# Unread products of the identity in TensorE's pauses of the first two blocks

## The chip, the cores and the metric

The kernel runs on one core of a Trainium2 chip. The metric is the time of one execution on the device in microseconds, median of three runs; lower is better. Besides, one execution was recorded by the hardware profiler, and all times of single instructions come from that one.

## What is computed

The reference has two halves. The first is attention within chunks of 64 positions; the second is a gated feed-forward layer on all 4608 rows.

```python
scores = q_c @ k_c.T / sqrt(64)              # per batch, head and chunk of 64
attn = softmax(scores)                        # exp, row sum + 1e-9, divide
x = (attn @ v_c)                              # laid out as 4608 rows of 512
g = x @ w_gate                                # 512 -> 1536
y = (g * sigmoid(g) * (x @ w_val)) @ w_out    # 1536 -> 512
```

There are 8 batches, 8 heads, 576 positions and a head dimension of 64.

## The kernel before, in words

The 4608 rows are worked in nine blocks of 512 (`NB`, `N`). For each block the kernel makes the attention output x, transposed, as four tiles of 128x512 (one for each pair of heads), and then for each of twelve slices f of 128 of the 1536 hidden columns a gate product, a value product and a projection back. To keep the accuracy of f32 at a better rate, each factor is split into a high and a low part in the type fp32r, and each product is made of three (`three`, lines 271 to 275: high times low, low times high, high times high). A gate or value product of one slice is thus twelve products of 128x128 by 128x512, recorded under lines 273, 274 and 275; a projection is twelve more under lines 318 to 320.

The weights come in as pairs of words and are first brought into f32 by a handful of steps on ScalarE and VectorE (`scale`, `sign`, `shift`, `below`, `power`, `weigh`, `join`, lines 74 to 97), then split by `upper` (line 124, ScalarE) and `lower` (line 129, VectorE).

The attention of the first two blocks, a0 and a1, is what matters here:

- `scores` (line 180) makes 64x64 products in plain f32 on quarters of the array (line 192) into two PSUM tiles; VectorE takes the row maximum (line 197) and subtracts it (line 198).
- `exponents` (line 201) is one ScalarE instruction for two pairs of heads; `normalize` (line 206) is four VectorE instructions, lines 208 to 211.
- `turn_by_pe` (line 213) turns a pair's probabilities by four 128x128 transposes with the identity (line 216) into a tile of ps_a, and ScalarE copies it out (line 217).
- `columns` (line 219) multiplies with v in 64x64 products (line 226) into a tile `px`.
- `split` (line 54) makes high (line 56, ScalarE) and low (line 57, VectorE) of px: these are the tiles xh and xl, which the gate's products read.

`by_pe` (line 395) does `turn_by_pe` and `columns` for two pairs. The identity `ident` (line 51) is filled by GpSimd at the start.

The order of the instructions on TensorE, ScalarE, VectorE and on the load queue is the order of the program text: lines 361 and 377 switch the planner off. So TensorE goes through lines 402 to 463 as they stand: scores of a0 in two halves, transposes and columns of a0 in two halves, first half of the scores of a1, the gate product of a0, second half of the scores of a1, the value product of a0, transposes and columns of a1 in two halves, gate and value products of a1, the first projection. An engine starts an instruction when the one ahead of it in its queue has started and its own data is there.

PSUM is divided by lines 46 to 48: `ps_gv` with two banks for gate and value, `ps_o` with four for the projection's sums (also lent to the scores' second half and to px in the first two blocks), `ps_a` with two for the attention.

Of the kernel before, what the change touches and what calls it, by code (L numbers as in the profile page):

```python
# [8 lines left out]
F32 = mybir.dt.float32  # L9
# [10 lines left out]
P = 128  # L20
# [15 lines left out]
def attn_then_gated_ffn(ctx: ExitStack, tc: tile.TileContext, qk, v, wgv, wo, out):  # L36
    nc = tc.nc
# [8 lines left out]
    ps_gv = ctx.enter_context(tc.tile_pool(name="ps_gv", bufs=2, space=bass.MemoryType.PSUM))  # L46
    ps_o = ctx.enter_context(tc.tile_pool(name="ps_o", bufs=T, space=bass.MemoryType.PSUM))
# [2 lines left out]
    const.tile([P, 96], F32, name="pad")  # L50
    ident = const.tile([P, P], F32, name="ident")
    make_identity(nc, ident)

    def split(src, hi, lo, engine=None):

        nc.scalar.copy(out=hi, in_=src)  # L56
        (engine or nc.vector).tensor_tensor(out=lo, in0=src, in1=hi.bitcast(F32), op=ALU.subtract)  # L57
# [225 lines left out]
    def product(a, f, g):  # L283
        ps = ps_gv.tile([P, N], F32, name="ps_gv")
        for kk in range(NK):
            three(ps, (w_hi[f][:, g, kk], w_lo[f][:, g, kk]), a.x[kk], kk, NK)
        return ps

    def gate(a, f):
        pg = product(a, f, 0)  # L290
        h = hp.tile([P, N], F32, name="h")
        nc.scalar.activation(h, pg, AF.Silu, scale=2.0 ** -8)  # L292
        return h

    def value(a, f):
        return product(a, f, 1)
# [102 lines left out]


    w, o = up[0], down[0]
    a0.scores(q0[0], 0)
    a0.scores(q0[1], 2, pool=ps_o, tag="ps_o")
    e = [a0.exponents(p, 2) for p in (0, 2)]
    w.scale()
    a0.normalize(e[0])
# [15 lines left out]


    a1.scores(q1[0], 0)
    h0 = gate(a0, 0)
    a1.scores(q1[1], 2, pool=ps_o, tag="ps_o")
    pv0 = value(a0, 0)
    w = up[1]
    w.scale()
    e = [a1.exponents(p, 2) for p in (0, 2)]  # L430
# [187 lines left out]
```

## Time and profile before

| what | before |
|---|---|
| median of 3 runs | 989.31 us (988.85 to 989.68) |
| profiled execution | 988.99 us |
| its span, first to last instruction | 987.1 us |
| mean granted clock of TensorE | 0.991 |
| TensorE busy, products | 952.7 us (97%), 6232 records |
| TensorE busy, weight loads | 782.2 us, 6232 records |
| VectorE busy | 513.5 us (52%) |
| ScalarE busy | 337.7 us (34%) |

In rows of the profile PE stands for TensorE's products, PEld for its weight loads, DVE for VectorE, ACT for ScalarE, POOL for GpSimd. A row of the timeline has start, length in us, engine, line, operation, output<-inputs and count; in brackets stands how long the engine had been idle and what released it. A row of a group has the total busy time and the mean of one in ns. A row of a stretch has its length, then the busy time (and count) of PE, PEld, DVE, ACT and POOL, the granted clock of TensorE (1.00 is full), the DMA share and GB/s. Ends of products are modelled, so lengths of single products overlap; what counts is the distance between starts.

### The profile page before, as it was taken

The numbers are of one execution on the slowest core, as the hardware profiler recorded it, in microseconds if no ns is written. First come the engines' busy times: TensorE is split into PE (matmuls) and PEld (weight loads), VectorE is DVE, ScalarE is ACT, GpSimd is POOL, SyncE is SP. The second block draws the span as 40 slices with busy tenths as digits, with TensorE's granted clock in tenths as the row PEclk, the third lists the DMA queues.
The fourth block names the chain that finished last, engine by engine and source line by source line (L and its number), as shares of the span: only waits on it lengthen the run. The fifth ranks groups of instructions, "written<-read, shape, count | busy, mean of one in ns | idle before, by whom it ended". The sixth has DMA issues, their size and how long they took to land.

```text
span 987.1 us, 14517 instructions
## 1 busy us (share of the span) xinstructions
PE 952.7 (97%) x6232; PEld 782.2 (79%) x6232; DVE 513.5 (52%) x816; ACT 337.7 (34%) x523; POOL 0.7 (0%) x6
## 2 busy tenths in 40 slices
PE   4689999999999999999999999999999999999998
PEld 4577888876888888888888888888888888888886
DVE  6777777758447524662356345633564347522221
ACT  3455444434532223222332323233322332223222
POOL 0000000000000000000000000000000000000000
PEclk9799999999999999999999999999999999999999
DMA  9061333235240005010401030002100120001001
GB/s 362 14 234 38 134 147 141 92 112 160 80 136 1 22 1 150 1 23 1 150 0 23 1 112 39 22 1 92 58 20 4 29 79 1 22 1 43 0 1 43
DMA packets 45600, 63.85 MB, mean 65 GB/s; under 512 B 29664, under 2 KB 29664, under 8 KB 44000
## 3 DMA queue, kind: packets, MB, share of 16 engines
q1 hardware_dynamic: 38624, 50.34, 15.8%
q10 hardware_dynamic: 6912, 12.59, 3.4%
q8 instruction: 49, 0.80, 0.3%
q14 instruction: 15, 0.12, 0.0%
HBM read 50.33 MB, written 12.58 MB: 64 GB/s over the span
## 4 chain that ended last, share of the span: by engine, by line
PE 91%; DVE 4%; DMA 2%; ACT 2%; issue 1%; ACTq 0%; SPq 0%; DVEq 0%
PE ps_gv L273 20%; PE ps_gv L274 19%; PE ps_gv L275 19%; PE ps_o L318 9%; PE ps_o L319 9%; PE ps_o L320 9%; DMA qk_t<-in_qk 2%; PE ps_a L192 2%; PE ps_a L251 1%; PE px L226 1%; DVE z L208 1%; DMA out<-o_sb 0%; DVE s_sb L211 0%; DVE t L81 0%; DVE t L97 0%
## 5 line engine op out<-in xcount | busy, mean ns | idle before, releaser
L273 PE MATMUL ps_gv<-xl,w 128*128 128x512 f32 x864 | 341.1, 395 | 3.4 <-ACT h L292 2.1
L274 PE MATMUL ps_gv<-xh,w 128*128 128x512 f32 x864 | 338.1, 391 | 3.2 <-DVE w L129 3.2
L275 PE MATMUL ps_gv<-xh,w 128*128 128x512 f32 x864 | 337.9, 391 | 0.0
L299 DVE SCALAR_TENSOR_TENSOR h<-ps_gv,h 128x512 f32<-128x512 f32 x108 | 74.6, 690 | 359.3 <-PE ps_gv L275 359.3
L273 PEld LDWEIGHTS ps_gv<-xl,w 128*128 128x128 f32 x864 | 163.0, 189 | 39.3 <-ACT h L292 2.5
L274 PEld LDWEIGHTS ps_gv<-xh,w 128*128 128x128 f32 x864 | 163.1, 189 | 36.9 <-DVE w L129 3.8
L275 PEld LDWEIGHTS ps_gv<-xh,w 128*128 128x128 f32 x864 | 163.0, 189 | 34.2
L292 ACT ACTIVATE h<-ps_gv 128x512 f32<-128x512 f32 x108 | 64.5, 597 | 315.0 <-PE ps_gv L275 314.9
L318 PE MATMUL ps_o<-woh,hl 128*128 128x512 f32 x432 | 169.9, 393 | 2.2 <-DVE hl L57 2.1
L319 PE MATMUL ps_o<-wol,hh 128*128 128x512 f32 x432 | 169.0, 391 | 0.0
L320 PE MATMUL ps_o<-woh,hh 128*128 128x512 f32 x432 | 168.9, 391 | 0.0
L56 ACT CAST hh<-h 128x512 fp32r<-128x512 f32 x96 | 59.6, 621 | 183.4 <-DVE h L299 183.4
L318 PEld LDWEIGHTS ps_o<-woh,hl 128*128 128x128 f32 x432 | 81.5, 189 | 21.1 <-issue 2.5
L319 PEld LDWEIGHTS ps_o<-wol,hh 128*128 128x128 f32 x432 | 81.6, 189 | 17.1 <-DVE wol L57 0.4
L320 PEld LDWEIGHTS ps_o<-woh,hh 128*128 128x128 f32 x432 | 81.5, 189 | 17.0
L238 DVE STREAM_TRANSPOSE turned<-s_sb 32x256 f32<-32x256 f32 x208 | 90.6, 436 | 3.1
L57 DVE TENSOR_TENSOR wol<-wo,woh 128x512 fp32r<-128x512 f32 x108 | 73.8, 683 | 12.8 <-ACT woh L56 12.8
L57 DVE TENSOR_TENSOR hl<-h,hh 128x512 fp32r<-128x512 f32 x96 | 66.4, 692 | 18.1 <-ACT hh L56 11.1
L56 ACT CAST woh<-wo 128x512 fp32r<-128x512 f32 x108 | 66.0, 611 | 11.1 <-DVE wo L97 11.1
L197 DVE TENSOR_REDUCE top<-ps_a 128x8 f32<-128x512 f32 x36 | 24.6, 685 | 36.1 <-PE ps_a L192 36.1
L192 PEld LDWEIGHTS ps_a<-qk_t 64*64 64x64 f32 x1152 | 20.4, 144 | 14.8 <-DMA qk_t<-in_qk 9.2
L192 PE MATMUL ps_a<-qk_t 64*64 64x64 f32 x1152 | 23.5, 232 | 8.8 <-DMA qk_t<-in_qk 8.4
(49 smaller groups left out, 438.7 us busy)
## 6 DMA issues: line engine op xcount, KB each, us to landing
qk_t<-in_qk SPq DMA_DIRECT2D x30, 512.0 KB, 4.5
raw<-in_wgv SPq DMA_DIRECT2D x12, 1024.0 KB, 7.0
out<-o_sb ACTq DMA_DIRECT2D x36, 256.0 KB, 2.3
raw<-in_wo SPq DMA_DIRECT2D x6, 1024.0 KB, 4.9
v_t<-in_v SPq DMA_DIRECT2D x26, 128.0 KB, 2.8
v_t<-in_v SPq DMA_DIRECT2D x52, 64.0 KB, 2.8
qk_t<-in_qk SPq DMA_DIRECT2D x3, 1024.0 KB, 13.8
h<-h ACTq DMA_DIRECT2D x12, 256.0 KB, 2.0
```

Of the source, the lines that this page charges most:

```text
L56: nc.scalar.copy(out=hi, in_=src)
L57: (engine or nc.vector).tensor_tensor(out=lo, in0=src, in1=hi.bitcast(F32), op=ALU.subtract)
L192: nc.tensor.matmul(ps[h][j * C:(j + 1) * C, i, u // 2, :], part[:, us:us + C], part[:, M * P + us:M * P + us + C], start=True, stop=True)
L238: nc.vector.transpose(out=self.turned[to:to + 32, p:p + 2, j, :, 32 * (i % 2):32 * (i % 2) + 32], in_=src[32 * i:32 * i + 32, :, o // 2, 3 ...
L273: nc.tensor.matmul(ps, wh, xl, start=k == 0, stop=False)
L274: nc.tensor.matmul(ps, wl, xh, start=False, stop=False)
L275: nc.tensor.matmul(ps, wh, xh, start=False, stop=k == n - 1)
L292: nc.scalar.activation(h, pg, AF.Silu, scale=2.0 ** -8)
L299: nc.vector.scalar_tensor_tensor(out=h, in0=pv, scalar=2.0 ** -8, in1=h, op0=ALU.mult, op1=ALU.mult)
L318: nc.tensor.matmul(o, hl[:, ts], woh, start=f == 0, stop=False)
L319: nc.tensor.matmul(o, hh[:, ts], wol, start=False, stop=False)
L320: nc.tensor.matmul(o, hh[:, ts], woh, start=False, stop=f == NF - 1)
```

## The change

A helper `keep_warm` is added. It takes a PSUM tile from a pool and issues n products of the identity with the identity into it, 128x128 by 128x128 in plain f32. Nothing reads the tile. It is called five times, and each call stands in TensorE's order where the text has it: 14 products ahead of the first scores of a0, 8 between their two halves, 50 between the scores and the transposes of a0, 48 between the first scores of a1 and the gate of a0, and 30 between the value product of a0 and the transposes of a1. The first four take their tile from `ps_gv`, the last from `ps_o`. Nothing is removed.

```diff
+    def keep_warm(n, pool, tag):
+
+        ps = pool.tile([P, P], F32, name="unread", tag=tag)
+        for _ in range(n):
+            nc.tensor.matmul(ps, ident, ident, start=True, stop=True)
...
     w, o = up[0], down[0]
+    keep_warm(14, ps_gv, "ps_gv")
     a0.scores(q0[0], 0)
+    keep_warm(8, ps_gv, "ps_gv")
     a0.scores(q0[1], 2, pool=ps_o, tag="ps_o")
+    keep_warm(50, ps_gv, "ps_gv")
     e = [a0.exponents(p, 2) for p in (0, 2)]
     w.scale()
     a0.normalize(e[0])
...
     a1.scores(q1[0], 0)
+    keep_warm(48, ps_gv, "ps_gv")
     h0 = gate(a0, 0)
     a1.scores(q1[1], 2, pool=ps_o, tag="ps_o")
     pv0 = value(a0, 0)
+    keep_warm(30, ps_o, "ps_o")
     w = up[1]
     w.scale()
     e = [a1.exponents(p, 2) for p in (0, 2)]
```

## Prediction

> **What bounds the kernel now.** I read the page first, then the timeline of TensorE over the first 90 us, then the busy time by stretches, then two groups of instructions and one line by itself. The page:
>
> ```profile
> span 987.1 us, 14517 instructions
> ...
> PE 91%; DVE 4%; DMA 2%; ACT 2%; issue 1%; ACTq 0%; SPq 0%; DVEq 0%
> ```
>
> TensorE carries 91% of the chain that ends last. The change touches only the first 60 us of it. The profiled execution took 988.99 us for a span of 987.1; the median of three runs is 989.31. My sum is made against 988.99.
>
> The timeline of TensorE (start, length, then what; in brackets the idle time before it and what ended it):
>
> ```profile
> 4.68 2.35 PE L192 MATMUL ps_a<-qk_t 64*64 64x64 f32 x64 [4.68 <-DMA qk_t<-in_qk]
> 8.38 1.99 PE L192 MATMUL ps_a<-qk_t 64*64 64x64 f32 x64 [1.35 <-DMA qk_t<-in_qk]
> 16.18 1.94 PE L216 MATMUL ps_a<-ident,s_sb 128*128 128x128 f32 x8 [5.82 <-DVE s_sb L211]
> 18.05 3.15 PE L226 MATMUL px<-pT,v_t 64*64 64x64 f32 x64
> 21.13 1.09 PE L216 MATMUL ps_a<-ident,s_sb 128*128 128x128 f32 x8
> 23.45 2.02 PE L226 MATMUL px<-pT,v_t 64*64 64x64 f32 x62 [1.23 <-ACT pT L217]
> ...
> 25.36 1.10 PE L192 MATMUL ps_a<-qk_t 64*64 64x64 f32 x62
> 27.46 0.50 PE L273 MATMUL ps_gv<-xl,w 128*128 128x512 f32 x1 [1.00 <-ACT w L124]
> 30.41 0.59 PE L274 MATMUL ps_gv<-xh,w 128*128 128x512 f32 x1 [2.44 <-DVE w L129]
> ...
> 34.72 1.16 PE L192 MATMUL ps_a<-qk_t 64*64 64x64 f32 x64
> 35.81 0.50 PE L273 MATMUL ps_gv<-xl,w 128*128 128x512 f32 x1
> ...
> 38.43 0.39 PE L275 MATMUL ps_gv<-xh,w 128*128 128x512 f32 x1
> 42.66 1.94 PE L216 MATMUL ps_a<-ident,s_sb 128*128 128x128 f32 x8 [3.84 <-DVE s_sb L211]
> 44.53 3.52 PE L226 MATMUL px<-pT,v_t 64*64 64x64 f32 x64
> ...
> 52.36 0.51 PE L273 MATMUL ps_gv<-xl,w 128*128 128x512 f32 x1
> ...
> 75.52 0.50 PE L273 MATMUL ps_gv<-xl,w 128*128 128x512 f32 x1 [2.11 <-ACT h L292]
> ```
>
> The reader is to see two things. First, the pauses: 3.3 us from the identity to the first scores, 1.35, 5.82, some 3.95 (from 26.46 to 30.41, with one product inside) and 3.84. Second, that the same work has two prices: eight transposes take 1.94 or 1.09, the 64 records of L192 2.0 or 1.1, those of L226 3.52 or 2.0. The busy time by stretches names the cause (the third figure from the right is the granted clock):
>
> ```profile
> 10.00:20.00 10.00, 4.18 (x60) 3.69 (x54) 9.27 (x14) 4.14 (x5) 0.00 (x0) 1.00 1.03 417
> ...
> 30.00:35.00 5.00, 4.59 (x28) 3.42 (x31) 2.93 (x5) 0.18 (x1) 0.00 (x0) 0.66 0.02 3
> ...
> 40.00:45.00 5.00, 2.34 (x16) 2.04 (x18) 4.79 (x8) 1.21 (x3) 0.00 (x0) 0.59 0.00 0
> 45.00:50.00 5.00, 4.71 (x89) 4.40 (x88) 3.36 (x7) 3.07 (x6) 0.00 (x0) 0.73 0.37 94
> ```
>
> Behind two of the pauses the clock drops to half for a while; 0.66 over 5 us is 3.4 us at half. Before 20 us the profile shows 1.00, yet the transposes at 16.18 take the same 1.94 as those at 42.66, so I take everything up to about 20 us as half clock too. That is what the change can win. What it costs is TensorE's own time for 150 products.
>
> **The price of one product of the identity.** No row of before has a plain 128x128 f32 product. The nearest are the transposes (same shape and type; the timeline, and all 40 with their least, median and longest time in ns) and, on the page, the plain f32 products of L192:
>
> ```profile
> 21.13 0.86 PEld L216 LDWEIGHTS ps_a<-ident,s_sb 128*128 128x128 f32 x8
> ```
>
> ```profile
> L216 PEld LDWEIGHTS ps_a<-ident,s_sb x40: 137/142/230, 16.2 to 237.1; 128*128 128x128 f32 x40
> L216 PE MATMUL ps_a<-ident,s_sb x40: 270/273/446, 16.2 to 237.2; 128*128 128x128 f32 x40
> ```
>
> ```profile
> L319 PEld LDWEIGHTS ps_o<-wol,hh 128*128 128x128 f32 x432 | 81.6, 189 | 17.1 <-DVE wol L57 0.4
> L320 PEld LDWEIGHTS ps_o<-woh,hh 128*128 128x128 f32 x432 | 81.5, 189 | 17.0
> ...
> L192 PE MATMUL ps_a<-qk_t 64*64 64x64 f32 x1152 | 23.5, 232 | 8.8 <-DMA qk_t<-in_qk 8.4
> ```
>
> One pass of a transpose: at full clock (1.09 - 0.273) / 7 = 0.117 us by the products, (0.86 - 0.142) / 7 = 0.103 by the weight loads of the same burst; I take 0.11. At half clock (1.94 - 0.446) / 7 = 0.213. How many passes? L192 is called 9 blocks x 4 pairs x 16 = 576 times and leaves 1152 records, so a plain f32 product is two records, while L216 has 40 calls and 40 records. Is the second weight load spared because the weights stay the same? L319 and L320 use the same stationary hh one behind the other, and both have 432 loads: no. So a product of the identity is two passes: 0.22 us at full clock, 0.427 at half. Bounds: two passes at 0.103 give 0.206; twice the 64-column pass of L226 ((2.02 - 0.22) / 30 = 0.06 for each pass of one of its two quadrants, so 0.12 for 128 columns) gives 0.24. If two passes were wrong and it is one, 0.11; that is a rival.
>
> The Trainium skill ("TensorE: Matmul & The Clock Gate", section "Back-to-back issue gap") puts an isolated 128-column product at 107 ns on a cold clock and about 56 on a warm one. By that the fifty would cost an estimated 2.8 to 5.4 us and fit their pause. The rows above do not bear it out for f32 operands: one pass of eight transposes alone is 0.11 warm.
>
> **The parts, in TensorE's order.** All five groups stand in TensorE's own queue, so whatever stands behind them waits, whether its data is there or not. They add no wait but one: the first group needs the identity, which GpSimd ends at 1.29:
>
> ```profile
> 1.00 0.29 POOL masks.py:199 TENSOR_SCALAR_AFFINE_SELECT ident<-ident 128x128 f32<-128x128 f32 x1
> ```
>
> Their banks cost nothing: four groups turn ps_gv round an even number of times, and the fifth takes the ps_o bank of the first block's third px, whose readers stand ahead of the gate. 600 more instruction records among 14517 I cost at nothing, at most 1 us if their loading shows.
>
> 1. *Fourteen.* From some 1.4 us (1.29 and an estimated 0.1) at half clock, 0.427 each. The clock rises after about one fully busy stretch of some 3.4 us (that behind 30.41), whose phase I can't know: somewhere between 4.8 and 8.2, say 6.5. Then 12 are done, two more take 0.44: end 6.95 (6.1 to 7.4). The first scores started at 4.68 in before, so they are now 2.3 late, but give way to the next work after 0.9 at full clock (1.10 less the last record's 0.2 of draining, mean 232 ns): 7.85.
> 2. *Eight*: 1.76 where the pause was: 9.6. Second scores 0.9: 10.5, with results at 10.7 against 10.37 before. VectorE starts on them 0.35 late, which moves the transposes' data from 16.18 to 16.5.
> 3. *Fifty*: 11.0 from 10.5 on, end 21.5; the data at 16.5 hides the first six. **The transposes start 5.3 late** (before 16.18).
> 4. From there to the end of the other block's first scores before took 26.46 - 16.18 = 10.3. Full clock saves 0.85 on the transposes and 1.1 on the first columns (3.15 to 2.02); VectorE and ScalarE have used the longer pause for their next steps and the transposes wait less for them, an estimated 0.6 of the 1.23 at 23.45. So 7.75: end 29.25, which is 2.8 late.
> 5. *Forty-eight*: 10.56, end 39.8. The weights' low half, for which the gate's second product waited at 30.41, would come about as late as the scores, at 33.2: the group hides that and goes 6.6 beyond. **The gate starts 9.4 late.**
> 6. Gate, scores and value: before 30.41 to 38.66 (38.43 and one more step of 0.23) = 8.25, the gate's 4.3 of it mostly at half clock. The value at full clock took 2.85 (35.81 to 38.66), the scores 1.09 (34.72 to 35.81): 2.85 + 1.09 + 2.85 = 6.8, end 46.6, 7.95 late.
> 7. *Thirty*: 6.6, end 53.2. The cover: after the value's end the transposes waited 4.0 us for VectorE's normalization in before (38.66 to 42.66), so 2.6 go beyond it. **10.55 late.**
> 8. Transposes and columns of the second block, 42.66 to 52.36 = 9.7: full clock saves 0.85 and 3.52 - 2.02 = 1.5, so 7.35: the next gate starts at 60.55. **8.2 late.**
>
> Do later pauses give it back? TensorE waits 2.11 at 75.52. But the chain of waits there runs through VectorE from the last split on:
>
> ```profile
> 53.08 0.69 DVE xl L57
> ```
>
> Behind it in VectorE's order stand the halves of h and of the output weights and the next weights' five steps; all start from columns that come 8.2 late. Nothing is given back. 988.99 + 8.2 = **997.2 us**.
>
> **The rivals.** (a) *A product is one pass*, 0.11. Then the fifty end at 16.0, in their pause; the forty-eight take 5.3 in 3.95, 1.35 over; the thirty take 3.3 in 4.0. The clock saves 1.45 at gate and value and 2.35 in the second block: 1.35 - 1.45 - 2.35 = -2.45, **986.5**, and with a badly placed rise of the clock up to 990. It decides below about 0.15 us per product: there the forty-eight go 3.25 and the thirty 0.5 over, as much as the clock's 3.8. For it: nothing in the rows; the shape is not in the trace. Against: 1152 records for 576 calls. 8 in 100. The skill's rule quoted above is a form of this rival.
> (b) *The identity's products don't raise the clock* (they are mostly zeros). Then all run at 0.427: the fifty take 21.3, the forty-eight 20.5, the thirty 12.8, and the real work between stays slow: some 46 us late (19.6 at the first transposes, 17.4 more at the gate, 9 more at the thirty), **1035**. Against: the transposes, whose one operand is the identity too, were followed by full clock at 21.13. 3 in 100.
> (c) *The change does nothing at the end*: the overruns meet work of VectorE and ScalarE that is the true bound, so that only 2 us or less remain, **989 to 991**. For: VectorE was busy 9.27 us of 10 to 20. Against: its next steps need columns that TensorE can't make before the fifty are through. 5 in 100.
>
> **How the numbers follow.** Forecast 84 in 100. Its own range: 0.206 or 0.24 per product moves 138 products at full clock by -1.9 or +2.8; the first rise of the clock -0.9 to +0.5; the saving of 0.6 in step 4 is an estimate, 0 to 1.2; a drop of the clock behind the first 100 us that falls otherwise is worth about 1.7, half of a stretch of 3.4. These don't all add up: 993.5 to 1001, which alone holds about 8 in 10. About 0.2% (2 us) is what a measurement of this kernel can tell from no change: slower by more 0.87 (the forecast and b), within 0.07 (c and part of a), faster 0.06 (the rest of a).
>
> **What would show it.** The 14, 50, 48 and 30 products as 28, 100, 96 and 60 records some 0.11 apart; transposes of the first block starting near 21.5 with no wait for VectorE, the gate near 40, the second transposes near 53, the gate of the second block near 60.5; a granted clock of 1.00 from about 7 to 70 us. Wrong: half as many records or half the spacing (a), a clock of 0.5 inside the groups (b), or transposes that still wait for VectorE behind the fifty (c).

## The result

The change is slower: 996.27 us (median of six, 994.60 to 997.83) against 989.15 (six, 988.85 to 989.72). The ratio is 1.007, with a 95% interval of 1.0056 to 1.0084. The profiled execution is the slowest of the six, 997.83 us with a span of 996.0.

On the page of the changed kernel the reader looks at the span, the granted clock in forty slices and the lines that make up the chain. Line numbers are six higher than before; L58 is the new product.

```profile
span 996.0 us, 15116 instructions
...
PEclk9999999999999999999999999999999999999999
...
PE ps_gv L279 19%; PE ps_gv L280 19%; PE ps_gv L281 19%; PE ps_o L324 9%; PE ps_o L325 9%; PE ps_o L326 9%; PE unread L58 4%; PE ps_a L198 2%; PE ps_a L257 1%; PE px L232 1%; DMA out<-o_sb 1%; DMA v_t<-in_v 0%; DMA qk_t<-in_qk 0%; ACT o_sb L331 0%; DVE hl L63 0%
```

Before, the same row of the clock had a drop in its second slice:

```profile
PEclk9799999999999999999999999999999999999999
```

Full clock now holds from about 7 us to beyond 70, and 4% of the chain that ends last are products that nobody reads. Not all of that is lost, since they also stand where TensorE would have waited. The timeline of TensorE shows where they stand past a pause:

```profile
1.36 6.12 PE L58 MATMUL unread<-ident 128*128 128x128 f32 x28 [1.36 <-POOL ident masks.py:199]
7.41 1.16 PE L198 MATMUL ps_a<-qk_t 64*64 64x64 f32 x64
8.50 2.05 PE L58 MATMUL unread<-ident 128*128 128x128 f32 x16
10.48 1.16 PE L198 MATMUL ps_a<-qk_t 64*64 64x64 f32 x64
11.57 11.43 PE L58 MATMUL unread<-ident 128*128 128x128 f32 x100
22.84 1.04 PE L222 MATMUL ps_a<-ident,s_sb 128*128 128x128 f32 x8
...
30.40 10.98 PE L58 MATMUL unread<-ident 128*128 128x128 f32 x96
41.15 0.48 PE L279 MATMUL ps_gv<-xl,w 128*128 128x512 f32 x1
...
48.00 6.86 PE L58 MATMUL unread<-ident 128*128 128x128 f32 x60
54.70 1.04 PE L222 MATMUL ps_a<-ident,s_sb 128*128 128x128 f32 x8
...
62.32 1.15 PE L232 MATMUL px<-pT,v_t 64*64 64x64 f32 x32 [1.21 <-DMA v_t<-in_v]
63.40 0.50 PE L279 MATMUL ps_gv<-xl,w 128*128 128x512 f32 x1
...
86.59 0.50 PE L279 MATMUL ps_gv<-xl,w 128*128 128x512 f32 x1 [2.11 <-ACT h L298]
```

No work behind the 28, 100, 96 and 60 records has an idle time in brackets: nothing waited for its data there, everything waited for TensorE. The same products by themselves (least, median and longest time in ns):

```profile
L58 PEld LDWEIGHTS unread<-ident x300: 186/192/333, 1.4 to 54.5; 128*128 128x128 f32 x150
L58 PE MATMUL unread<-ident x300: 270/275/580, 1.4 to 54.6; 128*128 128x128 f32 x150
```

150 products left 300 records and 300 weight loads, so each is two records (the prediction's "passes"), and no load of the unchanged weights was spared. From 11.57 to 22.84 there are 100 records and some 0.1 us of filling: 0.112 a pass, 0.223 a product.

### The profile page after: what moved, and what is told of

It reads as the page before. It is cut to its first block, busy times and chain, and to the rows that moved or that the text cites. A ratio compares the mean times of both kernels' runs of the same rounds, so it can differ in the third digit from the quotient of the medians.

```text
span 996.0 us, 15116 instructions
## 1 busy us (share of the span) xinstructions
PE 979.3 (98%) x6532; PEld 810.5 (81%) x6532; DVE 513.6 (52%) x816; ACT 337.9 (34%) x523; POOL 0.7 (0%) x6
## 4 chain that ended last, share of the span: by engine, by line
PE 93%; DVE 3%; ACT 2%; DMA 1%; issue 1%; ACTq 0%; SPq 0%; POOLq 0%; POOL 0%; DVEq 0%
PE ps_gv L279 19%; PE ps_gv L280 19%; PE ps_gv L281 19%; PE ps_o L324 9%; PE ps_o L325 9%; PE ps_o L326 9%; PE unread L58 4%; PE ps_a L198 2%; PE ps_a L257 1%; PE px L232 1%; DMA out<-o_sb 1%; DMA v_t<-in_v 0%; DMA qk_t<-in_qk 0%; ACT o_sb L331 0%; DVE hl L63 0%
## 5 line engine op out<-in xcount | busy, mean ns | idle before, releaser
L58 PE MATMUL unread<-ident 128*128 128x128 f32 x300 | 37.4, 289 | 1.4 <-POOL ident masks.py:199 1.4
L58 PEld LDWEIGHTS unread<-ident 128*128 128x128 f32 x300 | 36.7, 204 | 1.6 <-POOL ident masks.py:199 1.4
```

The source lines that it names most:

```text
L58: nc.tensor.matmul(ps, ident, ident, start=True, stop=True)
```

## The experiments

**The price halved.** The same counts, but of a copy of the identity in fp32r, of which a product is one record.

```diff
+    ident_r = const.tile([P, P], F32R, name="ident_r")
+    nc.vector.tensor_copy(out=ident_r, in_=ident)
...
-            nc.tensor.matmul(ps, ident, ident, start=True, stop=True)
+            nc.tensor.matmul(ps, ident_r, ident_r, start=True, stop=True)
```

> The same five groups with the same counts, but of an fp32r copy of the identity, so each product should be one pass of about 0.11 us in place of two (150 records in place of 300). Price theory (the loss is TensorE's own time for the products beyond each pause): the fifty end in their pause, the forty-eight go about 1.4 us over, the thirty fit; the next block's gate starts near 53 in place of 63.4, and the time is 987 to 990. Rival (the loss comes from the places, the banks taken or the added instructions, whatever a product costs): 150 added instructions of 300 stay, most of the 7 us stays, 993 to 996.

Measured: 990.14 us (987.79 to 991.45, ten), ratio 1.0013 (0.9995 to 1.003). Its timeline:

```profile
10.62 10.93 PE L60 MATMUL unread<-ident_r 128*128 128x128 f32 x50
21.34 1.93 PE L224 MATMUL ps_a<-ident,s_sb 128*128 128x128 f32 x8
...
30.43 5.58 PE L60 MATMUL unread<-ident_r 128*128 128x128 f32 x48
35.85 0.45 PE L281 MATMUL ps_gv<-xl,w 128*128 128x512 f32 x1
...
42.69 3.46 PE L60 MATMUL unread<-ident_r 128*128 128x128 f32 x30
...
46.60 1.09 PE L224 MATMUL ps_a<-ident,s_sb 128*128 128x128 f32 x8 [0.45 <-DVE s_sb L219]
...
55.29 0.50 PE L281 MATMUL ps_gv<-xl,w 128*128 128x512 f32 x1
```

The forty-eight and the thirty take half of what they took in the change, the transposes behind the thirty wait for VectorE again, and the loss of 7 us shrinks to about 1, which the interval can't tell from none; the median lies 0.14 above the expected range. The price theory holds; a cost of the places or of the added instructions as such would have left most of the loss. One part of the expectation missed: the fifty did not end in their pause. They took 0.214 each, the half-clock price, although TensorE had no pause from 8.70 to 23 (more on that at the end). So they took 10.7 us here (10.62 to 21.34), nearly the 11.3 of the change, and the next gate came at 55.29, not 53.

**One group left out.**

```diff
     a1.scores(q1[0], 0)
-    keep_warm(48, ps_gv, "ps_gv")
     h0 = gate(a0, 0)
```

> The change without the forty-eight. Price theory: these run 6.6 us beyond their cover, but they also keep the clock up for the gate behind them (about 1.5 us): the time falls by 5 us from the change's, to about 991. Rival (overruns meet work of VectorE and ScalarE that is the bound anyway): the time falls by less than 2 us.

Measured: 991.40 us (989.85 to 992.59, ten), ratio 1.003 (1.0015 to 1.0045); 4.9 below the change.

```profile
6.58 1.16 PE L198 MATMUL ps_a<-qk_t 64*64 64x64 f32 x64
...
33.39 0.79 PE L280 MATMUL ps_gv<-xh,w 128*128 128x512 f32 x1 [2.45 <-DVE w L135]
...
57.96 0.50 PE L279 MATMUL ps_gv<-xl,w 128*128 128x512 f32 x1
```

The wait for the weights' low half is back in its place, ending at 33.39; the prediction had put it at 33.2. The next gate is 5.4 earlier than in the change. Of that, 0.8 was there before the forty-eight: the first scores start at 6.58 here and at 7.41 in the change, because the fourteen took 5.30 in place of 6.12, the clock having risen earlier in this execution. Over the five kernels that have the fourteen and the eight unchanged, this start lies between 6.12 and 7.41, so starts in two traces are to be compared less that difference.

**The same group made longer**: 72 in place of 48.

> The change with 72 in place of the forty-eight. All 24 more stand beyond the cover: price theory 24 x 0.223 = 5.4 us more than the change, about 1001.6, a slope of one product's price each. Rival (cover): under 2 us more.

Measured: 1003.32 us (1002.75 to 1004.94, four), ratio 1.0159 (1.0128 to 1.019); 7.05 above the change, from another set of runs.

```profile
30.27 16.34 PE L58 MATMUL unread<-ident 128*128 128x128 f32 x144
46.37 0.48 PE L279 MATMUL ps_gv<-xl,w 128*128 128x512 f32 x1
...
68.24 0.50 PE L279 MATMUL ps_gv<-xl,w 128*128 128x512 f32 x1
```

The group itself grew by 16.34 - 10.98 = 5.36 us, exactly 24 products of 0.223, and the gate behind it came 5.2 later. The next gate is 4.84 later (68.24 against 63.40): nearly all of it is still there. The median lies 1.7 above the expected 1001.6, and the spans of the two profiled executions differ by 5.8. What comes on top of the 4.84 falls later and is not explained.

**The counts cut to the pauses.**

```diff
-    keep_warm(14, ps_gv, "ps_gv")
+    keep_warm(7, ps_gv, "ps_gv")
...
-    keep_warm(8, ps_gv, "ps_gv")
+    keep_warm(3, ps_gv, "ps_gv")
...
-    keep_warm(50, ps_gv, "ps_gv")
+    keep_warm(25, ps_gv, "ps_gv")
...
-    keep_warm(48, ps_gv, "ps_gv")
+    keep_warm(17, ps_gv, "ps_gv")
...
-    keep_warm(30, ps_o, "ps_o")
+    keep_warm(17, ps_o, "ps_o")
```

> The same five places with counts cut to the pauses: 7, 3, 25, 17 and 17 products (at 0.427 us in the first two, at 0.223 in the others: 3.0, 1.3, 5.6, 3.8, 3.8 us). Price theory: no overrun is left, the clock's saving stays: the next block's gate starts near 50 in place of 52.4, the time is 985.5 to 988.5. Rival (the places themselves cost): slower than the kernel before.

Measured: 984.67 us (981.85 to 987.39, ten), ratio 0.9962 (0.9945 to 0.9978). This beats the kernel before, by 4.4 us between the medians, and lies 0.8 below the expected range.

```profile
10.13 5.85 PE L58 MATMUL unread<-ident 128*128 128x128 f32 x50
16.02 1.06 PE L222 MATMUL ps_a<-ident,s_sb 128*128 128x128 f32 x8
...
23.27 3.53 PE L232 MATMUL px<-pT,v_t 64*64 64x64 f32 x61 [2.84 <-ACT pT L223]
...
31.54 0.47 PE L279 MATMUL ps_gv<-xl,w 128*128 128x512 f32 x1
...
42.32 1.09 PE L222 MATMUL ps_a<-ident,s_sb 128*128 128x128 f32 x8
...
50.43 0.50 PE L279 MATMUL ps_gv<-xl,w 128*128 128x512 f32 x1
...
73.59 0.50 PE L279 MATMUL ps_gv<-xl,w 128*128 128x512 f32 x1 [2.11 <-ACT h L298]
```

The places are the same; only the length differs. The transposes start at 16.02 (16.18 before), the second ones at 42.32 (42.66), and from there full clock carries the next gate to 50.43 (52.36). At the wait for h this kernel is 1.93 ahead (73.59 against 75.52). The one place that went wrong is 23.27: 2.84 us without work, the clock down, columns at half speed.

The lead of 1.93 does not last. Around the wait for h the clock drops once here (0.06 of 30 us, about 1.8); before, it was at 1.00 in every stretch from 50 to 200 us:

```profile
70.00:100.00 30.00, 27.89 (x116) 22.61 (x115) 22.36 (x33) 13.44 (x19) 0.00 (x0) 0.94 0.15 55
```

At the second scores of the first of the remaining attention blocks, the lead is 0.1 (208.02 against 208.12):

```profile
208.02 0.81 PE L198 MATMUL ps_a<-qk_t 64*64 64x64 f32 x32 [0.62 <-DMA qk_t<-in_qk]
209.16 0.69 PE L198 MATMUL ps_a<-qk_t 64*64 64x64 f32 x32 [0.32 <-DMA qk_t<-in_qk]
```

At their second half it is 1.74 (209.16 against 210.90): the kernel before waited 1.97 us there for a load, and had a drop of the clock behind it (its rows stand in the next section). So in the traces the 2.7 by which the spans differ arise at that place and not in the pauses that were filled. The changed kernel and the other seven of the experiments, slower or faster, waited only 0.21 to 0.34 there too. The one trace of the kernel before can't say whether its load is always that late, and what of the 4.4 is owed to the filled pauses stays open. Shown is that the cut counts took nothing from the first 75 us, where they saved 1.93.

**That place filled too**: ten more products between the first block's second transposes and their columns.

```diff
         for p in pairs:
             a.turn_by_pe(p, turned_by_pe[:, p])
+        if a is a0 and pairs[0] == 2:
+            keep_warm(10, ps_gv, "ps_gv")
```

> The counts cut to the pauses (7, 3, 25, 17, 17), and 10 more products in the pause between the first block's second transposes and their columns, 2.84 us long there, behind which the columns ran at half clock (3.53 us in place of 2.0) and the seventeen then ran 1.3 us past the weights. With the clock kept, the columns take 2.0, the gate starts at 30.2 in place of 31.5, and the time falls by about 1.3 us below the version with cut counts, to 983.4 (982.5 to 984.5 allowing for drops of the clock behind 200 us). If the clock drops all the same, or VectorE is the bound there, no difference: 984.7.

Measured: 982.74 us (982.40 to 984.94, six), ratio 0.9942 (0.9922 to 0.9962).

```profile
17.50 1.04 PE L222 MATMUL ps_a<-ident,s_sb 128*128 128x128 f32 x8
...
21.72 2.40 PE L58 MATMUL unread<-ident 128*128 128x128 f32 x20
24.11 2.02 PE L232 MATMUL px<-pT,v_t 64*64 64x64 f32 x61
...
30.88 0.48 PE L279 MATMUL ps_gv<-xl,w 128*128 128x512 f32 x1
```

The columns take 2.02 in place of 3.53, as expected. The gate came at 30.88, 0.7 later than expected and 0.66 earlier than with the cut counts. Part of that is the start: here the clock dropped once more ahead of the twenty-five, and the first block's transposes start at 17.50, not at 16.02. The two versions' intervals against the kernel before overlap, so the times alone do not tell them apart; this one has the lowest median of all.

**The first two groups alone, and the fifty alone.**

> Only the fourteen and the eight. Price theory: the second scores end 0.3 to 1.0 us later than before, VectorE hands that on to the first block, and nothing else changes: 989.3 to 990.3. Rival (the early rise of the clock pays for them): the time falls by 0.5 us or more below the kernel before.

Measured: 989.03 us (983.80 to 992.92, ten), ratio 1.0001 (0.9982 to 1.0021).

```profile
16.50 1.94 PE L222 MATMUL ps_a<-ident,s_sb 128*128 128x128 f32 x8 [5.82 <-DVE s_sb L217]
```

The transposes' data came at 16.50, the figure of step 2. The median lies 0.3 under the expected range and shows no gain either; in the total 0.3 us can't be seen, so the time does not tell the two theories apart.

> Only the fifty. They start at about 10.4 with the clock still at half, so the first 8 to 16 take 0.427 us: the transposes of the first block start at 23 to 25 in place of 16.18, the gate 4 to 5 us late, and the clock may drop again before it. Price theory: 992.5 to 994.5. Rival (cover: the steps behind are bound by VectorE): under 990.5.

Measured: 991.58 us (986.12 to 992.89, ten), ratio 1.0022 (1.0003 to 1.0041).

```profile
10.29 12.57 PE L58 MATMUL unread<-ident 128*128 128x128 f32 x100
22.70 1.04 PE L222 MATMUL ps_a<-ident,s_sb 128*128 128x128 f32 x8
...
34.07 0.80 PE L280 MATMUL ps_gv<-xh,w 128*128 128x512 f32 x1 [2.44 <-DVE w L135]
...
56.88 0.50 PE L279 MATMUL ps_gv<-xl,w 128*128 128x512 f32 x1
```

The transposes are 6.5 late, the gate's second product 3.7 and the next gate 4.5. Three expectations were a little too high: transposes at 23 to 25, 4 to 5 us at the gate, and a median 0.9 above the measured one. The loss is plain in the trace; in the total it is 2.6 us, and its interval begins just above none, so the time alone does not exclude the rival's 990.5; the 4.5 us at the next gate speak against it. Of the overrun of 6.5 us this block's own slack gives 2.8 back at the gate, where step 4 of the prediction had 2.5 (from 5.3 to 2.8).

**A wait that the prediction did not see.** In the change the second block's last columns waited 1.21 us for a tile of v, which can be loaded only when an earlier one has been read.

```diff
-    for p in range(NP):
+    for p in range(2):
         v1.append(ld.tile([P, 2 * T, C], F32, name="v_t"))
         nc.sync.dma_start(out=v1[p], in_=v[:, p, 1])
+    v23 = const.tile([P, 2, 2 * T, C], F32, name="v23", tag="w3")
+    nc.sync.dma_start(out=v23, in_=v[:, 2:4, 1])
+    v1 += [v23[:, 0], v23[:, 1]]
```

> The change, with the second block's third and fourth v tile loaded into the place of the first block's v as soon as that is read, so they don't wait for the first two tiles to come free. In the change the last columns of the second block waited 1.21 us for such a load, in step 8 of the prediction, which did not foresee it. If that wait holds up the chain, the next block's gate comes about 1.2 us earlier behind the thirty, near 8.0 us after the second transposes in place of 8.7, and the time is about 995. If something else is as late (ScalarE's copies and splits), the gate stays at 8.5 or more and the time within 0.5 us of the change.

Measured: 995.71 us (993.42 to 996.20, five), ratio 1.007 (1.0048 to 1.0093).

```profile
53.41 1.04 PE L222 MATMUL ps_a<-ident,s_sb 128*128 128x128 f32 x8
...
58.14 2.08 PE L232 MATMUL px<-pT,v 64*64 64x64 f32 x64 [0.29 <-ACT pT L223]
60.15 0.50 PE L279 MATMUL ps_gv<-xl,w 128*128 128x512 f32 x1
```

The wait is gone: the next gate follows the transposes after 6.74 us, in the change after 8.70, and 8.0 was expected. So in the trace the load did hold up the chain, by more than the 1.21. In the median only 0.56 us show, which the intervals can't tell from nothing; what became of the rest is open.

## Why the prediction was right, point by point

Forecast 997.2 us (993.5 to 1001.0), measured 996.27; the profiled execution took 997.83. The direction, the mechanism and the size hold; that the total comes so close is in part luck, as the last point shows.

| step | forecast, us | measured, us |
|---|---|---|
| 1: first scores start | 6.95 | 7.41 |
| 2: fifty start | 10.5 | 11.57 |
| 3: transposes start | 21.5 | 22.84 |
| 4: second block's first scores end | 29.25 | 30.47 |
| 5: gate starts | 39.8 | 41.15 |
| 6: thirty start | 46.6 | 48.00 |
| 7: second transposes start | 53.2 | 54.70 |
| 8: second block's gate starts | 60.55 | 63.40 |

- *The price* was 0.223 us at full clock where 0.22 was forecast; two records, no load spared. The first fourteen ended at 7.41, the upper end of the 6.1 to 7.4: their 28 records came 0.216 apart, so nearly all ran at half clock.
- *Steps 1 and 2*: the clock rose later than assumed (0.46), each of the two halves of the scores holds TensorE for 1.09 us (7.41 to 8.50), not 0.9, and the eight took 1.98 (8.50 to 10.48), not 1.76. Together these make the 1.1 by which the fifty start later than forecast.
- *Steps 3 to 7* lose another 0.4 together, mostly by the price.
- *Step 8* is the term that was mis-sized: 8.70 in place of 7.35. Columns at full clock came so early that they waited 1.21 for the load of v, for which those of the kernel before did not wait. With the load ahead of time the step took 6.74.
- *"Nothing is given back"* failed. At the wait for h the change stands 86.59 - 75.52 = 11.07 late, at the end 8.9. The place is behind 200 us, where the first of the remaining attention blocks is prepared. Before:

```profile
208.12 0.81 PE L192 MATMUL ps_a<-qk_t 64*64 64x64 f32 x32 [0.34 <-DVE o_sb L94]
210.90 0.69 PE L192 MATMUL ps_a<-qk_t 64*64 64x64 f32 x32 [1.97 <-DMA qk_t<-in_qk]
```

After, the second of them:

```profile
220.14 0.69 PE L198 MATMUL ps_a<-qk_t 64*64 64x64 f32 x32 [0.34 <-DMA qk_t<-in_qk]
```

And the stretches around them, before and after (granted clock in the third figure from the right):

```profile
205.00:220.00 15.00, 12.69 (x106) 10.10 (x106) 8.13 (x13) 4.93 (x6) 0.00 (x0) 0.89 0.44 141
```

```profile
215.00:230.00 15.00, 13.88 (x173) 10.98 (x164) 9.36 (x15) 6.46 (x8) 0.00 (x0) 1.00 0.41 141
```

TensorE waited 1.6 us less for a load, and one drop of the clock did not come (0.11 of 15 us, about 1.7). Some 1.1 of these 3.3 is lost again further on, where the changed kernel waits 1.20 for such a load at 392.49 and the kernel before does not; 2.2 remains. The forecast had a drop of the clock in its range, not in its sum. It is not the lateness that is given back: all eight kernels of the experiments wait at most 0.34 at the second of these rows, also the one with cut counts, which is not late there. What makes the load late in the trace of before is open. So the close agreement with the profiled execution is two misses that cancel by luck: 2.85 too little in the first 63 us, and 2.2 given back behind 200, for which the sum had nothing.

Of the rivals, (a) was decided by the records in the changed kernel's trace and by the run with one record a product, which brought the time back to 1 us of before. (b) fell in the trace: behind the fourteen, the eight ran at the full-clock price (16 records from 8.50 to 10.48). (c) fell with the 72: 5.36 us more of products, 5.2 us later gate.

The Trainium skill ("TensorE: Matmul & The Clock Gate", section "Back-to-back issue gap") gives about 56 ns for an isolated product of 128 columns on a warm clock, and about 81 for each product in a stream with its weight loads. Neither carries over to f32 here: a record takes 112, a product 223, four times the 56. The Trainium skill's page "FP8 and Floating Point Precision" (section "TensorE Precision Notes") counts four passes through the array for true FP32. The trace shows two records a product and does not show what is inside one. That four times 56 comes near the 223 does not decide it, since an fp32r product of one record also took 0.113 at full clock (forty-eight from 30.43 to 35.85).

## What to carry to other kernels

Filler work on an in-order engine is priced by the shape and type that is really issued, record by record, and compared with the pause as the trace shows it; 150 products of 0.223 us in pauses of 18 us cost 7, while 69 of them, cut to the same pauses, cost nothing and left the kernel 1.9 us ahead at 75 us. A gain in the total is to be followed to the place where it arises: of the 4 us of that version, the trace puts the part it shows behind 200 us. The pause to compare with is that of the changed schedule: here the pauses moved with the delays and kept their length (without the forty-eight, the wait for the weights' low half ended at 33.39 in place of 30.41 and was 2.45 us long, 2.44 before), and work made faster by the clock can run into a load that was hidden before.

## What was not expected of the hardware

- Busy is not enough to raise the clock. Fp32r products of 128 columns, one record each, ran at 0.214 us apiece for 10.7 us without a pause, the half-clock price all through; in the kernel with the fifty alone the f32 products, which started on the same low clock, took 12.57 us for twice as many records, where half clock throughout would make 21.3. At full clock the fp32r products kept it (5.58 us for forty-eight). Why the one kind raises the clock and the other does not is open.
- Products of which nearly all operands are zeros do raise the clock: behind the fourteen, the eight took 2.05 us for 16 records, the full-clock price, in all five kernels that have both groups unchanged.
- Single times of one kernel spread further than the first runs showed: 25 runs of the kernel before, taken beside the experiments, lie between 983.62 and 992.33 us. Drops of the clock behind 70 us, about 1.7 us each, come at different places in the traces and may be part of that: the fastest of the 25 has a mean granted clock of 0.996, the slowest of 0.990.
